# Feed-forward products that stream their columns from last to first

## The chip, the core and the metric

The kernel runs on one core of a Trainium2 chip. Its time is the device time of one execution in microseconds (us). Beside the times there is a profile of one execution: every instruction of the engines TensorE (PE for its products, PEld for the loads of their stationary operand), VectorE (DVE), ScalarE (ACT), GpSimd (POOL) and the queue of SyncE (SP), with its start and its duration, and the DMA transfers.

## The reference

Two steps follow each other. The first is attention over short windows: sequences of 768 positions are cut into chunks of 32, and each chunk attends to 8 memory keys, 16 positions to its left, itself and 8 positions to its right. The second is a feed-forward layer over 3072 tokens with 512 features and 2048 hidden units, in float32:

```python
for c in range(nc):                       # chunks of 32 positions
    k_full = np.concatenate([mem_k, k_ctx], axis=2)
    scores = scale * np.matmul(q_c, k_full.transpose(0, 1, 3, 2))
    ...                                   # softmax: a
    out[:, :, c_start:c_end] = np.matmul(a, v_full)

def _moe_ref(x, w_in, w_out):             # x: 3072 x 512
    h = x @ w_in                          # 3072 x 2048
    g = np.where(h >= 1, h, np.where(h <= -1, 0.0, (h + 1) ** 2 / 4))
    return g @ w_out                      # 3072 x 512
```

## The kernel before

The 3072 tokens are cut into six blocks of 512 (`TB`). The 2048 hidden units are cut into 16 groups of 128, so there are 96 steps, one for each block and group. A step has two sets of products on TensorE:

- the **hidden products** (`pe_hidden`, and the same lines in `early_step`): 128 hidden units of 512 tokens are summed in one PSUM tile `ps_h`. The stationary operand is a 128x128 piece of the weights `wr`, the moving operand is x transposed: 128 features by 512 tokens.
- the **output products** (`pe_products`): the stationary operand is 128x128 of the gated hidden units, `gh` or `gl`, the moving operand 512 columns of `wr`; four tiles `ps_o`, one for each 128 tokens of the block, gather the sum over the 16 groups.

Float32 accuracy comes from splitting each operand in a high part and a remainder (`xth` and `xtl`, `gh` and `gl`, and two halves of `wr`), so that each product is done three times: high by high, high by remainder, remainder by high. A hidden step has 3 x 4 products (4 pieces of 128 features), an output step 3 x 4 (4 tiles of tokens). In the first two blocks some steps are done on half a block: their hidden products have 256 moving columns, and their output steps 6 products.

Between the two sets, ScalarE and VectorE work on one tile of 128x512: two `Relu` and a `Square` on ScalarE, a min-and-add on VectorE, a cast to `gh` on ScalarE and a subtraction to `gl` on VectorE. The output products of a step are issued two steps later (`LAG`). The attention of later blocks (`ps_s` scores, `ps_x` values) is put between the steps, and so is, in the first blocks, the decoding of the packed weights.

All engines run their instructions in the order in which the code issues them (`InOrder`); for the first two blocks this order is the written list `FIRST`, afterwards the loop over steps. All engine calls pass through line 63, so in the profile every instruction has that line, and the groups are told apart by their tiles. In the rows, `ps_h<-xth,wr` and `ps_h<-xtl,wr` are hidden products, `ps_o<-wr,gh` and `ps_o<-wr,gl` output products. Of the kernel's products, `ps_s`, `ps_x`, the transposes `ps_h<-ident,pr` and eight products on zeros at the start (`ps_h<-warm`) are issued by other lines.

Of the kernel before, what the change touches and what calls it, by code (L numbers as in the profile page):

```python
# [16 lines left out]
P = 128  # L17
# [32 lines left out]
"""  # L50

LAST = 2


class InOrder:
# [13 lines left out]
def attn_ffn_kernel(ctx: ExitStack, tc: tile.TileContext, first_qk, first_v, qk, vw, w, out):  # L69
    nc = tc.nc  # L70
    engines = (nc.tensor, nc.scalar, nc.vector, nc.gpsimd, nc.sync)
    pe, act, dve, pool, sp = (InOrder(tc, e) for e in engines)
# [6 lines left out]
    NFC = NPW  # L79
# [14 lines left out]
    def two_banks(tag, name):  # L94
        return ps_2.tile([P, 2, 512], F32, name=name, tag=tag)
# [43 lines left out]
    def weights(which, fc, part):  # L139
        i, j = place[which, fc]  # L140
        c0 = part * n2 + j * DM
        return ws[i][:, c0 : c0 + DM]
# [250 lines left out]
    def hidden_terms(wh, wl, xh, xl):  # L393
        return [(m, x, cc) for m, x in ((wh, xh), (wl, xh), (wh, xl)) for cc in range(NP)]

    def pe_products(outs, gh, gl, wh, wl, fc):

        kinds = list(enumerate(((gh, wh), (gh, wl), (gl, wh))))
        todo = [(t, kind) for kind in kinds for t in range(len(outs))]
        if fc == NFC - 1:  # L400
            todo.sort(key=lambda x: x[0])
        for t, (i, (g, m)) in todo:
            ts = slice(t * P, (t + 1) * P)
            pe.matmul(outs[t], g[:, ts], m, start=fc == 0 and i == 0, stop=fc == NFC - 1 and i == 2)

    def pe_hidden(s):
        blk, fc = divmod(s, NFC)
        xh, xl = xts[blk]
        hp = hidden[s] = ps_h.tile([P, 512], F32, name="ps_h")
        wh, wl = weights(0, fc, 0), weights(0, fc, 1)  # L410
        terms = hidden_terms(wh, wl, xh, xl)
        for n, (m, x, cc) in enumerate(terms):
            pe.matmul(hp, m[:, cc * P : (cc + 1) * P], x[:, cc], start=n == 0, stop=n == len(terms) - 1)

    def gating(s):

# [24 lines left out]
    def pe_out(s):  # L441
        blk, fc = divmod(s, NFC)
        gh, gl = gs.pop(s)
        if fc == 0:
            pairs = [two_banks(f"a{i}", "ps_o") for i in range(NT // 2)]
            acc[blk] = [pairs[t // 2][:, t % 2] for t in range(NT)]
        wh, wl = weights(1, fc, 0), weights(1, fc, 1)
        pe_products(acc[blk], gh, gl, wh, wl, fc)
# [3 lines left out]
    def early_step(name, blk, tokens, fc):  # L452

        items.append(name)
        size = len(tokens) * P
        xh, xl = (x[:, :, tokens[0] * P : tokens[0] * P + size] for x in xts[blk])
        n = 0
        if size < TB:
            n = len(halves) % 2
            halves.append(name)  # L460
        hp = ps_h.tile([P, 512], F32, name="ps_h")[:, 0:size]
        wh, wl = weights(0, fc, 0), weights(0, fc, 1)
        terms = hidden_terms(wh, wl, xh, xl)
        for i, (m, x, cc) in enumerate(terms):
            pe.matmul(hp, m[:, cc * P : (cc + 1) * P], x[:, cc], start=i == 0, stop=i == len(terms) - 1)
        yield
        if n == 0:
            tiles = (
                gpool.tile([P, TB], F32, name="gw", tag="gw"),
                gpool.tile([P, TB], F32, name="gt"),  # L470
                gpool.tile([P, TB], F32R, name="gh", bufs=3),
                gpool.tile([P, TB], F32R, name="gl", bufs=3),
            )
            if size < TB:
                both["g"] = tiles
        else:
            tiles = both["g"]
        g, t, gh, gl = (x[:, n * HT : n * HT + size] for x in tiles)
        act.activation(g, hp, AF.Relu, bias=0.5, scale=0.5)
        act.activation(t, hp, AF.Relu, bias=-1.0)  # L480
        act.activation(g, g, AF.Square)
        yield
        dve.scalar_tensor_tensor(g, g, 1.0, t, op0=ALU.min, op1=ALU.add)
        yield
        act.copy(gh, g)
        yield
        dve.tensor_tensor(gl, g, gh.bitcast(F32), op=ALU.subtract)
        yield
        if fc == 0:
            acc.setdefault(blk, [None] * NT)  # L490
            pair = two_banks(f"a{tokens[0] // 2}", "ps_o")
            for t in tokens:
                acc[blk][t] = pair[:, t % 2]
        wh, wl = weights(1, fc, 0), weights(1, fc, 1)
        pe_products([acc[blk][t] for t in tokens], gh, gl, wh, wl, fc)
        yield
        if fc < NFC - 1:
            return
        for t in tokens:
            if t % 2 == 0:  # L500
                ob = apool.tile([P, 2, DM], F32, name="ob", tag="f", bufs=2)
            (act.copy if t % 2 else dve.tensor_copy)(ob[:, t % 2], acc[blk][t])
            r0 = blk * TB + t * P
            sp.dma_start(out[r0 : r0 + P, :], ob[:, t % 2])
            yield
# [45 lines left out]
    for name in FIRST.split():  # L551
        if name == "+":
            load, *which = next(early)
            load(*which)
            continue
        if name not in chains:
            kind, i = name[0], int(name[1:])
            chains[name] = early_step(name, *parts[kind], i) if kind in parts else kinds[kind](i)
        next(chains[name])
# [13 lines left out]
    for s in range(first * NFC, steps):  # L573
# [22 lines left out]
        if k_scores is not None:  # L596
            act.activation(prob[k_scores], prob[k_scores], AF.Exp, scale=SCALE)
        pe_hidden(s)
        gating(s)
        if s - LAG >= first * NFC:  # L600
# [3 lines left out]
        else:  # L604
            n, i = LAST // LAG, s - first * NFC
            for name in items[len(items) - LAST :][i * n : (i + 1) * n]:
                for _ in chains[name]:
# [96 lines left out]
```

## Time and profile before

| what | value |
|---|---|
| three runs | 608.14, 608.02, 608.13 us (median 608.13) |
| span of the profiled execution, first to last instruction | 606.4 us |
| its time outside the span | no row gives it; the median of the runs lies 1.7 us above the span |
| PE, busy | 591.0 us (97% of the span), 5496 products |
| PEld, busy | 483.7 us (80%) |
| DVE, busy | 325.6 us (54%) |
| ACT, busy | 281.2 us (46%) |
| mean granted TensorE clock | 0.986 |

A product's row on PE has its duration from start to modelled end, and the products of a stream overlap: the mean duration is longer than the distance from one start to the next. The pace of a stream is therefore read from the timeline, from the start of one group of products to the start of the next, divided by their number. In a timeline row the first number is the start, the second the length of the merged piece, and the last the number of instructions.

### The profile page before, as it was taken

The numbers are of one execution on the slowest core, as the hardware profiler recorded it, in microseconds if no ns is written. First come the engines' busy times: TensorE is split into PE (matmuls) and PEld (weight loads), VectorE is DVE, ScalarE is ACT, GpSimd is POOL, SyncE is SP. The second block draws the span as 40 slices with busy tenths as digits, with TensorE's granted clock in tenths as the row PEclk, the third lists the DMA queues.
The fourth block names the chain that finished last, engine by engine and source line by source line (L and its number), as shares of the span: only waits on it lengthen the run. The fifth ranks groups of instructions, "written<-read, shape, count | busy, mean of one in ns | idle before, by whom it ended". The sixth has DMA issues, their size and how long they took to land.

```text
span 606.4 us, 12265 instructions
## 1 busy us (share of the span) xinstructions
PE 591.0 (97%) x5496; PEld 483.7 (80%) x5496; DVE 325.6 (54%) x466; ACT 281.2 (46%) x503; POOL 0.7 (0%) x6
## 2 busy tenths in 40 slices
PE   5889999999999999999999999999999999999996
PEld 2888888888888888888888888888888888888885
DVE  5999999987483224736424734623553632322222
ACT  2689764544444434344434434434433343533342
POOL 0000000000000000000000000000000000000000
PEclk8699999999999999999999999999999999999999
DMA  8999200433131004012201213101310000100001
GB/s 353 423 418 420 124 1 1 175 110 137 31 145 70 1 0 175 30 42 105 70 1 73 103 70 106 70 1 54 121 70 2 1 2 0 70 0 1 0 1 69
DMA packets 9845, 55.31 MB, mean 91 GB/s; under 512 B 1089, under 2 KB 1089, under 8 KB 5185
## 3 DMA queue, kind: packets, MB, share of 16 engines
q1 hardware_dynamic: 9792, 54.53, 23.2%
q8 instruction: 43, 0.70, 0.5%
q14 instruction: 10, 0.07, 0.0%
HBM read 48.23 MB, written 6.29 MB: 90 GB/s over the span
## 4 chain that ended last, share of the span: by engine, by line
PE 94%; DVE 3%; ACT 1%; DMA 1%; issue 0%; DVEq 0%; ACTq 0%
PE ps_o L63 44%; PE ps_h L63 44%; PE ps_x L63 3%; PE ps_s L63 3%; DVE f L63 1%; DMA qk<-in_first_qk_dram 1%; DVE pr L63 1%; DVE mx L63 0%; DVE den L63 0%; ACT w L63 0%; ACT gw L63 0%; DVE wr L63 0%; DVE xtl L63 0%; ACT pr L63 0%; ACT wr L63 0%
## 5 line engine op out<-in xcount | busy, mean ns | idle before, releaser
L63 PE MATMUL ps_o<-wr,gh 128*128 128x512 f32 x768 | 199.5, 396 | 0.0
L63 PE MATMUL ps_h<-xth,wr 128*128 128x512 f32 (+1 forms) x832 | 197.3, 379 | 0.0
L63 PEld LDWEIGHTS ps_h<-xth,wr 128*128 128x128 f32 x832 | 148.7, 189 | 31.9 <-DVE wr L63 0.5
L63 PEld LDWEIGHTS ps_o<-wr,gh 128*128 128x128 f32 x768 | 143.7, 188 | 32.5
L63 DVE SCALAR_TENSOR_TENSOR gw<-gw,gt 128x512 f32<-128x512 f32 (+1 forms) x104 | 67.2, 648 | 170.0 <-ACT gw L63 169.5
L63 ACT ACTIVATE gw<-ps_h 128x512 f32<-128x512 f32 (+1 forms) x104 | 58.7, 564 | 167.8 <-PE ps_h L63 167.7
L63 PE MATMUL ps_o<-wr,gl 128*128 128x512 f32 x384 | 109.0, 394 | 0.0
L63 PE MATMUL ps_h<-xtl,wr 128*128 128x512 f32 (+1 forms) x416 | 105.2, 375 | 0.0
L63 DVE TENSOR_TENSOR gl<-gw,gh 128x512 fp32r<-128x512 f32 (+1 forms) x104 | 67.4, 649 | 67.4 <-ACT gh L63 67.3
L63 ACT CAST gh<-gw 128x512 fp32r<-128x512 f32 (+1 forms) x104 | 61.1, 590 | 68.7 <-DVE gw L63 68.7
L63 PEld LDWEIGHTS ps_h<-xtl,wr 128*128 128x128 f32 x416 | 75.3, 190 | 14.1
L63 PEld LDWEIGHTS ps_o<-wr,gl 128*128 128x128 f32 x384 | 72.5, 189 | 17.2
L63 ACT ACTIVATE gw<-gw 128x512 f32<-128x512 f32 (+1 forms) x104 | 62.5, 601 | 0.0
L63 ACT ACTIVATE gt<-ps_h 128x512 f32<-128x512 f32 (+1 forms) x104 | 58.2, 559 | 0.0
L63 DVE STREAM_TRANSPOSE pt<-pr 32x512 f32<-32x512 f32 (+1 forms) x60 | 41.2, 698 | 1.3
L63 DVE SCALAR_TENSOR_TENSOR f<-w,f 128x1024 uint32<-128x1024 uint32 x32 | 38.9, 1220 | 0.4
L63 PEld LDWEIGHTS ps_x<-pt,v 64*64 64x64 f32 x1536 | 25.2, 142 | 5.5 <-issue 3.5
L63 ACT ACTIVATE pr<-pr 128x1024 f32<-128x1024 f32 (+1 forms) x14 | 13.1, 937 | 35.5 <-DVE pr L63 35.4
L63 PE MATMUL ps_x<-pt,v 64*64 64x32 f32 x1536 | 26.7, 226 | 1.6 <-ACT pt L63 1.6
L63 ACT CAST xth<-ps_x 128x512 fp32r<-128x512 f32 x24 | 13.1, 590 | 21.6 <-PE ps_x L63 21.5
L63 PEld LDWEIGHTS ps_s<-qk 64*32 64x32 f32 x1536 | 16.7, 110 | 6.4 <-issue 3.2
L63 ACT CAST wr<-f 128x1024 fp32r<-128x1024 f32 x16 | 16.8, 1050 | 9.3 <-DVE f L63 9.3
(27 smaller groups left out, 182.1 us busy)
## 6 DMA issues: line engine op xcount, KB each, us to landing
w<-in_w_dram SPq DMA_DIRECT2D x16, 1024.0 KB, 19.8
qk<-in_qk_dram SPq DMA_DIRECT2D x10, 1536.0 KB, 6.7
v<-in_vw_dram SPq DMA_DIRECT2D x10, 1024.0 KB, 5.1
out_dram<-ob SPq DMA_DIRECT2D x24, 256.0 KB, 2.0
qk<-in_first_qk_dram SPq DMA_DIRECT2D x4, 768.0 KB, 8.8
v<-in_first_v_dram SPq DMA_DIRECT2D x4, 512.0 KB, 12.8
```

Of the source, the lines that this page charges most:

```text
L63: return self.tc.keep_in_program_order(getattr(self.engine, name)(*args, **kwargs))
```

## The change

A helper `products` issues a product with the columns of the moving operand in descending order, and with the columns of the PSUM output in the same descending order. Column c of the output is still the product with column c of the moving operand. The hidden products (both places) and the output products go through it; the stationary operand is read as before. The instructions of every engine, their order and their waits are the same in both kernels; the two access patterns of each of these products start at the last column and have the step -1 instead of 1. Lines below the helper move down by five, so that line 63 becomes line 68.

```diff
+def products(pe, out, stationary, moving, **flags):
+
+    pe.matmul(out[:, ::-1], stationary, moving[:, ::-1], **flags)
+
+
...
 def pe_products(outs, gh, gl, wh, wl, fc):
...
-            pe.matmul(outs[t], g[:, ts], m, start=fc == 0 and i == 0, stop=fc == NFC - 1 and i == 2)
+            products(pe, outs[t], g[:, ts], m, start=fc == 0 and i == 0, stop=fc == NFC - 1 and i == 2)
...
 def pe_hidden(s):
...
-            pe.matmul(hp, m[:, cc * P : (cc + 1) * P], x[:, cc], start=n == 0, stop=n == len(terms) - 1)
+            products(pe, hp, m[:, cc * P : (cc + 1) * P], x[:, cc], start=n == 0, stop=n == len(terms) - 1)
...
 def early_step(name, blk, tokens, fc):
...
-            pe.matmul(hp, m[:, cc * P : (cc + 1) * P], x[:, cc], start=i == 0, stop=i == len(terms) - 1)
+            products(pe, hp, m[:, cc * P : (cc + 1) * P], x[:, cc], start=i == 0, stop=i == len(terms) - 1)
```

## The prediction, as written before the result

> **What bounds the kernel now.** I read the page's first part, then the chain of work that ended last, then what PE waits for. Rows of the page:
>
> ```profile
> span 606.4 us, 12265 instructions
> PE 591.0 (97%) x5496; PEld 483.7 (80%) x5496; DVE 325.6 (54%) x466; ACT 281.2 (46%) x503; POOL 0.7 (0%) x6
> PE 94%; DVE 3%; ACT 1%; DMA 1%; issue 0%; DVEq 0%; ACTq 0%
> PE ps_o L63 44%; PE ps_h L63 44%; PE ps_x L63 3%; PE ps_s L63 3%; DVE f L63 1%; DMA qk<-in_first_qk_dram 1%; DVE pr L63 1%; DVE mx L63 0%; DVE den L63 0%; ACT w L63 0%; ACT gw L63 0%; DVE wr L63 0%; DVE xtl L63 0%; ACT pr L63 0%; ACT wr L63 0%
> ```
>
> The chain is PE for 94% of the span, and the two tiles that the change touches, `ps_o` and `ps_h`, hold 88% of it. PE's waits, as the view of waits lists them in full:
>
> ```profile
> PE ps_h L63 <- DVE pr L63: 6.6, 3, 4.1
> PE ps_x L63 <- ACT pt L63: 1.6, 1, 1.6
> PE ps_s L63 <- DMA qk<-in_first_qk_dram: 1.4, 3, 0.8
> PE ps_h L63 <- DVE warm L63: 1.2, 1, 1.2
> ```
>
> Together they are 10.8 us, and none of them is in front of a feed-forward product: `ps_h <- DVE pr` is the transposes of attention, which also land in `ps_h`. So whatever a feed-forward product gains or loses in pace goes into the time in full. The windows of 100 us show the same from the other side:
>
> ```profile
> core 0: us, PE busy (x) PEld busy (x) DVE busy (x) ACT busy (x) POOL busy (x), PEclk, DMA share, GB/s
> 200.00:300.00 100.00, 100.00 (x913) 81.36 (x912) 45.82 (x65) 41.37 (x74) 0.00 (x0) 1.00 0.18 64
> 400.00:500.00 100.00, 100.00 (x913) 81.33 (x913) 45.41 (x65) 41.41 (x75) 0.00 (x0) 1.00 0.11 38
> ```
>
> PE is never idle there, at the full granted clock (1.00), while DVE and ACT are busy less than half of the time and DMA less than a fifth. The other engines could follow products that were 2% faster, and they are covered by products that are slower.
>
> **The pace of a product** is the quantity that the change can move. One late step in the timeline of PE, and one early stretch with the attention out of the way:
>
> ```profile
> 490.50 2.01 PE L63 MATMUL ps_h<-xth,wr 128*128 128x512 f32 x8
> 492.35 1.08 PE L63 MATMUL ps_h<-xtl,wr 128*128 128x512 f32 x4
> 493.26 2.03 PE L63 MATMUL ps_o<-wr,gh 128*128 128x512 f32 x8
> 495.13 1.09 PE L63 MATMUL ps_o<-wr,gl 128*128 128x512 f32 x4
> 496.06 0.40 PE L63 MATMUL ps_h<-xth,wr 128*128 128x512 f32 x1
> ```
>
> ```profile
> 45.50 1.11 PE L63 MATMUL ps_h<-xth,wr 128*128 128x256 f32 x8
> 46.45 0.64 PE L63 MATMUL ps_h<-xtl,wr 128*128 128x256 f32 x4
> 46.93 0.39 PE L63 MATMUL ps_o<-wr,gh 128*128 128x512 f32 x1
> ...
> 51.10 1.98 PE L63 MATMUL ps_h<-xth,wr 128*128 128x512 f32 x8
> 52.92 1.08 PE L63 MATMUL ps_h<-xtl,wr 128*128 128x512 f32 x4
> 53.83 1.10 PE L63 MATMUL ps_o<-wr,gh 128*128 128x512 f32 x4
> ```
>
> From start to start: 12 late hidden products take 493.26 - 490.50 = 2.76 us, 230.0 ns each; 12 late output products 496.06 - 493.26 = 2.80 us, 233.3 ns each. The 12 hidden products from 51.10 take 2.73 us, 227.5 ns each, the fastest stretch of this shape that I found. Twelve products of 256 columns take 46.93 - 45.50 = 1.43 us, 119.2 ns each. Between 256 and 512 columns lie 227.5 - 119.2 = 108.3 ns, so a column costs 108.3 / 256 = 0.423 ns, and what doesn't grow with the columns is 227.5 - 512 x 0.423 = 10.9 ns. A product is thus 95% stream of columns. The counts come from the groups by shape, the loads of the stationary operand beside them:
>
> ```profile
> L63 PE MATMUL ps_o<-wr,gh 128*128 128x512 f32 x768 | 199.5, 396 | 0.0
> L63 PE MATMUL ps_h<-xth,wr 128*128 128x512 f32 x704 | 178.3, 395 | 0.0
> L63 PE MATMUL ps_o<-wr,gl 128*128 128x512 f32 x384 | 109.0, 394 | 0.0
> L63 PE MATMUL ps_h<-xtl,wr 128*128 128x512 f32 x352 | 94.7, 391 | 0.0
> L63 PE MATMUL ps_h<-xth,wr 128*128 128x256 f32 x128 | 19.1, 294 | 0.0
> L63 PE MATMUL ps_h<-xtl,wr 128*128 128x256 f32 x64 | 10.5, 288 | 0.0
> L63 PEld LDWEIGHTS ps_h<-xth,wr 128*128 128x128 f32 x832 | 148.7, 189 | 31.9 <-DVE wr L63 0.5 <-issue 0.2
> L63 PEld LDWEIGHTS ps_o<-wr,gh 128*128 128x128 f32 x768 | 143.7, 188 | 32.5
> ```
>
> That is 1152 output products, 1056 hidden products of 512 columns and 192 of 256. By the late paces they take 1152 x 233.3 = 268.8 us, 1056 x 230.0 = 242.9 us and 192 x 119.2 = 22.9 us, together 534.6 us: 88% of the span, as the chain has it. So the paces describe the whole run. The load of 188 or 189 ns does not set them: the 256-column products follow each other every 119.2 ns with loads of the same kind, so a load's duration overlaps its neighbours.
>
> **The change part by part.** It adds no instruction, removes none, moves none, and moves no wait: the order on each engine is the same row for row. The stationary operand is loaded as before (no cost). What differs in 2400 products is the direction in which columns are read from SBUF and written to PSUM. Three things can have a price.
>
> First, *the boundary between two products*. Today a hidden product's four pieces of x lie behind one another, so the next product begins where the last one ended, except at every fourth. The output products jump back: four of them in a row read the same 512 columns of `wr`. This is the nearest the trace comes to a price of where a stream begins: 233.3 against 230.0 and 227.5 ns. With the change, all hidden products jump too (from the first column of a piece to the last column of the next). From below the price is a gain of 233.3 - 227.5 = 5.8 ns on output products and 2.5 ns on hidden ones, if the jump in the new direction is free and the small irregularity of the pace goes with it: 1152 x 5.8 + 1056 x 2.5 = 6.7 + 2.6 = 9.3 us. From above I take the fixed part of a product paid once more: 2400 x 10.9 ns = 26.2 us. The value that I take is 0. The output tiles' jump goes along with a change of the PSUM tile at every product, so the difference of 3.3 ns need not be the jump's; and in the 12 products from 51.10 the eight of `xth` take 1.82 us and the four of `xtl` 0.91 us, 227.5 ns each, although the stream jumps back after every fourth.
>
> Second, *the stream itself*. From below, 0 per column: the four products that share a moving operand, operands in 16 weight tiles and x tiles of alternating blocks all stream within 3% of each other, so what counts is how many columns there are. From above: the columns come one by one where now two come in the same time. The nearest row with such a pace is that of the first products of all, bf16 ones on zeros:
>
> ```profile
> 1.19 3.59 PE L63 MATMUL ps_h<-warm 128*128 128x512 bf16 x8 [1.19 <-DVE warm L63]
> L63 PE MATMUL ps_h<-warm 128*128 128x512 bf16 x8 | 3.6, 630 | 1.2 <-DVE warm L63 1.2
> ```
>
> The last of the eight starts 3.59 - 0.63 = 2.96 us after the first, 423 ns apiece or 0.826 ns a column, nearly twice 0.423. At 2208 x 512 + 192 x 256 = 1,179,648 columns, a further 0.826 - 0.423 = 0.403 ns is 475 us, and a further 0.423 ns is 499 us. I take 0: nothing in the rows makes a stream depend on its place, and a step of -1 touches the same words as a step of 1, each once, neighbours after neighbours. But every product in this trace runs upward, so no row measures it, and both ends stay for the chances.
>
> [...]
>
> Third, *who waits for the end*. Nobody reads part of a product's output: ScalarE's first `Relu` follows the last of 12 hidden products, the stores the last output product. The order inside changes nothing for them. Cost 0.
>
> The sum is 0 + 0 + 0 against the profiled span of 606.4 us, which lies 1.7 us under the median of the runs; I carry that distance over. Forecast: 608.1 us.
>
> **The rivals.**
>
> *Descending streams run at half the rate* (the far side: slower). Place: every feed-forward product, on reading x and `wr` or on writing `ps_h` and `ps_o`. Price: 499 us by doubling the column, 475 us by the warm-up row, so 1083 to 1107 us. It decides from the first hidden product near 24 us on, since PE has no idle time in which to hide it. For it: the ascending stream takes 0.423 ns a column, half of the 0.826 ns that TensorE also shows, so two columns are handled in the time of one, and pairing may be built for rising addresses alone. Against: only that pairing by place would work both ways. [...]
>
> *A small cost at each product* (slower). The hidden products lose their run-on from piece to piece and take the output products' pace: 1056 x 3.3 ns = 3.5 us, 611.6 us; with a whole fixed part more for each product, 26.2 us, 634.3 us. For it: output products, which jump at every boundary, are the slower kind. Against: the early jumps at every fourth hidden product, which cost nothing visible.
>
> *A small gain.* The 3.3 to 5.8 ns by which late products lie above 227.5 come from how a stream meets its surroundings and go away in the other direction: up to 9.3 us, 598.8 us. For it: the same hidden products take 227.5 ns at 51 us and 230.0 ns at 490 us, so these nanoseconds aren't part of the product. Against: nothing says that direction is what they depend on.
>
> *The change does nothing*: both patterns reversed describe the same set of pairs of columns, and if the instruction were normalised, the chip would see the old one. Time 608.1 us; it falls together with the forecast.
>
> **How the numbers follow.** A difference of 0.2%, 1.2 us, is about the least that a measurement of this kernel tells from no change. No measurable difference (with the rival of a change that does nothing): 0.50. Small gain: 0.15. Small cost: 0.15. Half rate: 0.20. Faster is thus 0.15, the same 0.50, slower 0.15 + 0.20 = 0.35. The range from 598 to 634 us holds the first three, 0.80, with the bounds of 598.8 and 634.3; what it leaves out is the half rate. The forecast's own range is 606.9 to 609.3 us.
>
> **What would show it.** If the forecast holds: late steps with 2.76 us for hidden and 2.80 us for output products, mean durations of 391 to 396 ns in the groups, and PE's waits as above. A small cost or gain: the distance of starts in these same late steps, and only there; 256-column products shifted by the same nanoseconds as those of 512 columns if it lies at the boundary, by half as much if it lies in the columns. Half rate: starts some 440 ns apart, loads with gaps of more than 200 ns between them, DVE and ACT near a quarter. The forecast is wrong if the span moves by more than 1.2 us; its reason is wrong if the paces move and cancel.

## The result, and the profile after

The changed kernel takes 612.3 us (612.31 and 612.35, a third run 614.03) where the kernel before takes 608.1. The ratio over all three is 1.0078, with an interval of 1.0064 to 1.0092. Measured again beside the experiments it was 612.35 against 608.15 us, 1.0069 (1.0054 to 1.0084). The change costs 4 us, 0.7%. One run each of this kernel and of the experiments `d2_pad_down` and `b1_read` took 832.33, 832.82 and 652.92 us at granted clocks of 0.65 to 0.84 and is left out of all numbers; the rows below are of a second profile of the changed kernel, `a1_both`.

The page of the changed kernel, span, engines and chain:

```profile
span 610.5 us, 12349 instructions
PE 595.2 (97%) x5496; PEld 483.2 (79%) x5496; DVE 325.8 (53%) x466; ACT 281.4 (46%) x503; POOL 0.7 (0%) x6
PE 94%; DMA 4%; ACT 1%; SPq 0%; issue 0%; DVE 0%; DVEq 0%; ACTq 0%
```

The page counts 84 instructions more than that of the kernel before (12349 against 12265). In the trace they are semaphore instructions of some 51 ns in TensorE's queue, one more in nearly every hidden step. So the instructions of the two kernels are not quite the same, against what the section on the change says. The experiments show that they cost nothing: `b2_write`, `b3_halves` and `b4_fours` have the same 12349 and take the time of the kernel before, while `b1_read` with 12265 and `a3_output` with 12264 have the whole loss.

The span grows by 4.1 us and PE's busy time by 4.2 us. PE's waits are as they were:

```profile
PE ps_h L68 <- DVE pr L68: 6.7, 3, 4.1
PE ps_x L68 <- ACT pt L68: 1.6, 1, 1.6
PE ps_h L68 <- DVE warm L68: 1.2, 1, 1.2
PE ps_s L68 <- DMA qk<-in_first_qk_dram: 1.0, 2, 0.8
```

They sum to 10.5 us against 10.8. So no wait appeared; the products themselves are slower. PE's timeline shows where, in a late step of the changed kernel and 16 steps on:

```profile
504.92 2.03 PE L68 MATMUL ps_h<-xth,wr 128*128 128x512 f32 x8
506.78 1.10 PE L68 MATMUL ps_h<-xtl,wr 128*128 128x512 f32 x4
507.72 2.03 PE L68 MATMUL ps_o<-wr,gh 128*128 128x512 f32 x8
509.58 1.10 PE L68 MATMUL ps_o<-wr,gl 128*128 128x512 f32 x4
510.52 1.80 PE L68 MATMUL ps_h<-xth,wr 128*128 128x512 f32 x7
...
594.52 2.03 PE L68 MATMUL ps_h<-xth,wr 128*128 128x512 f32 x8
```

Hidden and output products both take 2.80 us for twelve: 233.3 ns each. Sixteen steps take 594.52 - 504.92 = 89.60 us, 5.600 us a step. The kernel before, over the same 16 steps:

```profile
501.61 2.01 PE L63 MATMUL ps_h<-xth,wr 128*128 128x512 f32 x8
...
590.46 2.01 PE L63 MATMUL ps_h<-xth,wr 128*128 128x512 f32 x8
```

88.85 us, 5.553 us a step. The 2208 products of 512 columns are worth 2208 / 24 = 92 such steps: 92 x 0.047 = 4.3 us. The products of 256 columns went the other way, a little. Early, in the changed kernel:

```profile
45.42 1.11 PE L68 MATMUL ps_h<-xth,wr 128*128 128x256 f32 x8
46.37 0.64 PE L68 MATMUL ps_h<-xtl,wr 128*128 128x256 f32 x4
46.84 0.63 PE L68 MATMUL ps_o<-wr,gh 128*128 128x512 f32 x2
```

That is 1.42 us for twelve, 118.3 ns each, against 119.2 ns (1.43 us) before: over 192 products 0.2 us less. By these samples 4.3 - 0.2 = 4.1 us, the growth of the span. Summed over all starts in the records, the distances behind hidden products of 512 columns grew by 3.7 us and those behind output products by 0.7 us; those behind products of 256 columns fell by 0.1 us and those behind all others by 0.2 us.

The starts of the single products say more than their mean. The distances from one start to the next in a step of each kernel, the ones from 501.61 and from 504.92 us, in ns, from the records (12 hidden products, then 12 output products):

```
before, hidden   236 224 231 236 228 232 231 227 227 226 227 232
before, output   241 233 231 231 229 230 232 241 232 231 232 233
after,  hidden   234 233 233 234 233 233 234 233 233 234 233 233
after,  output   234 233 233 234 233 233 234 233 233 234 233 233
```

Before, the pace is uneven in the same way in nearly every step; the hidden products settle at 226.7 ns after some seven products, the output products never settle and repeat a pattern of seven with a mean of 232.4. After, every product takes 233.3. The change replaced a mixture with a mean of 231.4 by a constant that is a little worse.

### The profile page after: what moved, and what is told of

Its sections match the earlier page's. It is cut to its first block, busy times and chain, and to the rows that moved or that the text cites. A ratio compares the mean times of both kernels' runs of the same rounds, so it can differ in the third digit from the quotient of the medians.

```text
span 830.5 us, 12349 instructions
## 1 busy us (share of the span) xinstructions
PE 816.0 (98%) x5496; PEld 541.4 (65%) x5496; DVE 327.9 (39%) x466; ACT 281.9 (34%) x503; POOL 0.7 (0%) x6
## 4 chain that ended last, share of the span: by engine, by line
PE 97%; DVE 2%; DMA 1%; ACT 0%; issue 0%; DVEq 0%; ACTq 0%
PE ps_h L68 46%; PE ps_o L68 45%; PE ps_x L68 4%; PE ps_s L68 2%; DMA qk<-in_first_qk_dram 1%; DVE f L68 0%; DVE pr L68 0%; DVE den L68 0%; DVE mx L68 0%; DVE wr L68 0%; DVE ob L68 0%; ACT gw L68 0%; DVE rin L68 0%; ACT pr L68 0%; ACT pt L68 0%
## 5 line engine op out<-in xcount | busy, mean ns | idle before, releaser
L68 PE MATMUL ps_o<-wr,gh 128*128 128x512 f32 x768 | 272.5, 511 | 0.0
L68 PE MATMUL ps_h<-xth,wr 128*128 128x512 f32 (+1 forms) x832 | 269.5, 486 | 0.0
L68 PEld LDWEIGHTS ps_h<-xth,wr 128*128 128x128 f32 x832 | 168.5, 214 | 81.8 <-issue 24.6
L68 PEld LDWEIGHTS ps_o<-wr,gh 128*128 128x128 f32 x768 | 159.7, 209 | 87.8 <-issue 28.0
L68 PE MATMUL ps_o<-wr,gl 128*128 128x512 f32 x384 | 148.3, 503 | 0.0
L68 PE MATMUL ps_h<-xtl,wr 128*128 128x512 f32 (+1 forms) x416 | 143.6, 475 | 0.0
L68 PEld LDWEIGHTS ps_h<-xtl,wr 128*128 128x128 f32 x416 | 83.6, 211 | 42.4 <-issue 14.7
L68 PEld LDWEIGHTS ps_o<-wr,gl 128*128 128x128 f32 x384 | 78.1, 203 | 46.6 <-issue 16.7
L68 PEld LDWEIGHTS ps_x<-pt,v 64*64 64x64 f32 x1536 | 32.5, 176 | 7.0 <-issue 5.1
L68 PE MATMUL ps_x<-pt,v 64*64 64x32 f32 x1536 | 34.0, 245 | 0.9 <-ACT pt L68 0.9
L68 DVE COPY ob<-ps_o 128x512 f32<-128x512 f32 (+1 forms) x16 | 9.6, 622 | 37.9 <-PE ps_o L68 37.9
```

What stands on the lines that cost most here:

```text
L68: return self.tc.keep_in_program_order(getattr(self.engine, name)(*args, **kwargs))
```

## The experiments

### Which products, and where they begin

The first four runs separate the two theories that the prediction left: a price at the boundary between products, or one in the stream. Each kernel is the changed one with one edit. `a1_both` is the changed kernel itself.

> The changed kernel itself, for a profile at the clock of the kernel before. The boundary theory (each hidden product loses the run-on from one piece of x to the next): +3 to +5 us, the distance of starts in late hidden products up from 230.0 to about 233 to 234 ns, late output products unchanged at 233.3 ns, the attention's products unchanged. The stream theory (each column read or written downward costs a little more): about 1.8 ns more on every 512-column product, 231.8 ns hidden and 235.1 ns output, and 0.9 ns more on those of 256 columns.

Measured: 612.35 us, the rows above. Hidden products at 233.3 ns fit the boundary theory, and so do output products, whose mean is unchanged; but the 256-column products became faster, which fits neither.

`a2_hidden`:

```diff
 def pe_products(outs, gh, gl, wh, wl, fc):
-            products(pe, outs[t], g[:, ts], m, ...)
+            pe.matmul(outs[t], g[:, ts], m, ...)
```

> Only the hidden products run downward; output products upward as before. Boundary theory: the whole loss, +3 to +5 us. Stream theory: the share of the hidden products' columns, 590,000 of 1,180,000, so half the loss, about +2.1 us.

Measured: 612.2 us (one of four runs 613.66), ratio 1.0072 (1.0057 to 1.0087). The hidden products alone bring the whole loss.

`a3_output`: `products` in `pe_products` only, `pe.matmul` in both hidden places.

> Only the output products run downward. Boundary theory: no loss, within 0.5 us of the kernel before, because their stream already jumps at each boundary. Stream theory: half the loss, about +2.1 us.

Measured: 613.0 us, ratio 1.0079 (1.0062 to 1.0096). The output products alone bring the whole loss too. Both theories miss: one wanted 0, the other 2.1 us. The step of this run on PE:

```profile
505.45 2.01 PE L68 MATMUL ps_h<-xth,wr 128*128 128x512 f32 x8
507.30 1.08 PE L68 MATMUL ps_h<-xtl,wr 128*128 128x512 f32 x4
508.22 2.06 PE L68 MATMUL ps_o<-wr,gh 128*128 128x512 f32 x8
510.11 1.11 PE L68 MATMUL ps_o<-wr,gl 128*128 128x512 f32 x4
511.06 0.39 PE L68 MATMUL ps_h<-xth,wr 128*128 128x512 f32 x1
```

Here the downward output products take 2.84 us for twelve, 236.7 ns, where the same products take 233.3 when the hidden ones run downward too. The losses do not add up: 4.1 and 4.9 us apart, 4.2 together.

`a4_pieces`, the changed kernel with:

```diff
-    ... for cc in range(NP)]
+    ... for cc in reversed(range(NP))]
```

> All products run downward as in the changed kernel, and the four pieces of x are taken from the last to the first, so that a downward hidden product ends where the next one begins, as the upward ones do in the kernel before. The sums are the same with another order of terms. Boundary theory: the loss is gone, within 0.5 us of the kernel before. Stream theory: the same loss as the changed kernel, +4 to +5 us.

Measured: 612.36 us, 1.0069 (1.0054 to 1.0084), the same loss, although each downward hidden product but every fourth now ends where the next one begins. The boundary theory falls.

### Reading or writing, and what "downward" means

`b1_read` and `b2_write` turn only one side of each product:

```diff
-    pe.matmul(out[:, ::-1], stationary, moving[:, ::-1], **flags)
+    pe.matmul(out, stationary, moving[:, ::-1], **flags)      # b1_read
+    pe.matmul(out[:, ::-1], stationary, moving, **flags)      # b2_write
```

> The moving operands are read downward, the outputs written upward. The columns of each product therefore land mirrored (tokens within a block, features in the output), with the same number of products and words; that part of the result is another one. Read theory (the price lies in reading SBUF downward, together with the load of the next stationary operand from the same memory): the whole loss, +4 us, 233.3 ns in late hidden and output products, evenly. Write theory (the price lies in writing PSUM downward): the time of the kernel before, with its uneven paces (226 to 241 ns).

> The moving operands are read upward as in the kernel before, the outputs written downward, so that columns land mirrored as well. Read theory: the time of the kernel before and its uneven paces. Write theory: +4 us with 233.3 ns evenly. If each gives half of it, neither holds.

Measured: reading downward 612.43 us, 1.0071 (1.0054 to 1.0088); writing downward 608.07 us, 1.0000 (0.9990 to 1.0009). The price lies in reading alone. In the run that writes downward, a step has the distances of the kernel before within 1 ns (the one from 501.55 us begins 236 224 231 236 228 233 230 227). So writing the output with a step of -1 cost nothing here.

`b3_halves` takes the second half of the columns first, each half upward; `b4_fours` turns the columns inside each group of four (16 bytes), the groups upward:

```diff
+    a, b = (x.rearrange("p (h c) -> p h c", c=n)[:, ::-1] for x in (out, moving))     # b3_halves, n = half
+    a, b = (x.rearrange("p (h c) -> p h c", c=4)[:, :, ::-1] for x in (out, moving))  # b4_fours
+    pe.matmul(a, stationary, b, **flags)
```

> Read and written upward, but the second half of the columns ahead of the first, by one instruction with two runs of columns. If the direction decides (step -1 from column to column), this keeps the time and the pace of the kernel before, but for a jump in the middle. If the place decides at which a stream is while the next stationary operand is loaded, the pace changes as much as in the changed kernel, by 3 ns or more a product.

> Groups of four columns (16 bytes) go upward, and inside each group the columns go downward, in reading and in writing. If the step from word to word decides, the loss of the changed kernel stays, +4 us, or more. If only the large order decides (which part of the operand is read when), the kernel takes the time of the kernel before. If a turn inside a group costs time, which neither kernel has, the stream slows by tens of ns a product and the time by 50 us or more.

Measured: 608.11 us, 1.0000 (0.9991 to 1.0010), and 608.14 us, 0.9999 (0.9990 to 1.0009). In `b4_fours` every single step from word to word inside a group is -1, and it costs nothing. So it isn't the step of words inside 16 bytes that has a price: with the groups of 16 bytes in downward order as well the kernel takes 612.35 us.

### The pace of single kinds of products

To ask many such questions at once, `c1_probe` is the kernel before with 26 stretches of 36 products each behind its end (819.4 us in all), `c2_probe` the same in the opposite order (820.9 us). The core of a stretch, shortened; `offset` counts columns of 4 bytes:

```python
for i in range(36):
    a = i % 3
    s = wh[:, a * 128 : a * 128 + cols]                  # or wh[:, ::4]
    m = xh[:, a * 512 + offset : a * 512 + offset + n]
    pe.matmul(hp[0:cols, 0:n], s, order(m), start=True, stop=True)
```

> The kernel before, and behind its last product 26 stretches of 36 products each, whose results nobody reads; only their pace is asked, from start to start, and the whole time is longer by them. Each stretch changes one thing: the direction of the moving operand, the number of columns of the stationary operand (128, 64, 32), the number of moving columns (512, 256), the address of the moving operand (later by 16, 64 or 256 bytes), a stationary operand taken from every fourth word, groups of columns turned round (inside groups of 16, 64 and 256, or groups of 4, 16 and 64 in downward order), bf16 operands. Collision theory (a downward stream meets the load of the next stationary operand in SBUF more often): 226.7 ns up and 233.3 ns down at 128 stationary columns, the difference below 2 ns at 32 columns, whose load is a quarter; other paces with the strided load, and with at least one of the shifted addresses. Own-price theory (a downward product pays some 6.7 ns by itself, whatever is loaded beside it): the same difference of 6 to 7 ns at 128, 64 and 32 columns, in bf16 too, and no effect of the stride and the addresses.

> The same 26 stretches in the opposite order. If the pace of a stretch belongs to the stretch, each has the pace that it had in the other order within 1 ns. If it depends on what went before, as the output products' pace seems to (233.3 ns where the hidden products run downward too, 236.7 ns where they run upward), some of them change by 3 ns or more.

Measured, mean of the last 24 distances of starts of each stretch in ns, from the records of both runs; the two runs agree within 0.1 ns (where the trace lacks a record, as it does in one bf16 stretch of each run, the other run's number stands), so a stretch's pace is its own and not its predecessor's:

| stretch (512 columns, 128 stationary columns where not said) | up | down |
|---|---|---|
| plain | 226.7 | 233.3 |
| the same operands every time | 226.7 | 233.3 |
| 64 stationary columns | 230.0 | 233.3 |
| 32 stationary columns | 231.7 | 233.3 |
| stationary operand from every fourth word | 235.0 | 233.3 |
| moving operand 16 bytes later | 231.7 | 233.3 |
| moving operand 64 bytes later | 228.9 | 233.3 |
| moving operand 256 bytes later | 226.7 | 233.3 |
| 256 moving columns | 120.0 | 118.3 |
| bf16 | 215.8 | 215.8 |

| order of the columns | |
|---|---|
| inside groups of 4 downward (from `b4_fours`) | as up |
| inside groups of 16 downward, groups upward | 266.7 |
| inside groups of 64 or 256 downward, groups upward | 233.3 |
| groups of 4 or of 16 in downward order, upward inside | 233.3 |
| groups of 64 in downward order, upward inside | 226.7 |

Rows of PE's timeline in `c1_probe`, upward: part of the plain stretch, then of the one whose stationary operand is every fourth word:

```profile
602.27 6.97 PE L63 MATMUL ps_h<-xth,wr 128*128 128x512 f32 x30
...
732.80 5.57 PE L63 MATMUL ps_h<-xth,wr 128*128 128x512 f32 x23
```

Less 0.39 and 0.40 us for the last product's own duration, 29 distances of the first row take 6.58 us, 226.9 ns each (its first ones are not settled), and 22 of the second 5.17 us, 235.0 ns.

Three things follow. First, the upward pace is not a property of the product alone: it goes from 226.7 to 235.0 ns when only the stationary operand changes (every fourth word; with 64 or 32 columns, 230.0 and 231.7 ns, the output has fewer rows as well) and to 231.7 or 228.9 ns when only the moving operand's address does (16 or 64 bytes later). The difference of 6.7 ns falls to 1.7 at 32 columns, as the collision theory said, yet not in the way that it said: up becomes slower, down stays. So it is no simple count of meetings with a shorter load, and the load of a quarter of the columns was not a quarter as long: 109 ns against 188. Nor is it the length of the load alone: every fourth word takes 309 ns to load beside upward products and 312 ns beside downward ones, whose pace stays at 233.3 ns. Second, in these stretches the downward pace of 512 columns is 233.3 ns with every stationary operand and address that was tried; in the kernel of `a3_output` it was 236.7. Third, with groups in downward order but upward inside, groups of 4 and 16 columns have the downward pace, 233.3 ns, and groups of 64 (256 bytes) the upward one, 226.7 ns. Groups of 32 columns were not tried, and groups of 16 turned inside, at 266.7 ns, have neither pace.

bf16 products show no difference, in the one place that was tried: 215.8 ns in either direction. In float32 a change of the stationary operand alone moved the upward pace from 226.7 to 235.0 ns; what the product loses there, no run shows.

### The shift that beats both kernels

The stretches suggest a reason for the output products' uneven 232.4 ns in the kernel before. In the built programs' addresses, x and the weights begin at 1664 modulo 2048, so that a hidden product's two operands lie whole multiples of 512 bytes apart, the distance of the plain stretch. The tiles of `gh` and `gl` begin at 0 modulo 2048, 128 bytes off. `d1_pad_up` puts 128 unused bytes ahead of their pool; `d2_pad_down` does the same in the changed kernel:

```diff
+    gpool.tile([P, 32], F32, name="pad", bufs=1)
     warm = gpool.tile([P, DM], BF16, name="warm", tag="gw")
```

> The kernel before, products upward, with 128 unused bytes ahead of the pool that holds gh and gl. In the kernel before, those tiles begin 128 bytes off a multiple of 512 from the weights, while x and the weights lie whole multiples of 512 bytes apart. Collision theory (the upward pace hangs on where the moving operand and the next stationary operand lie to one another): the output products settle at 226.7 ns instead of their uneven 232.4, and the hidden products behind them have no slow start; 1152 x 5.7 = 6.6 us and up to 1056 x 3 = 3.2 us less, 598 to 602 us. Own-price theory, and any theory in which the output products are slower because they change the PSUM tile: no change, 608.1 us.

> The changed kernel, products downward, with the same 128 bytes. Collision theory as the stretches bear it out (every downward stretch settled at 233.3 ns, whatever its addresses): 612.3 us, no change against the changed kernel. If the downward pace hangs on the addresses as well, it moves by 3 us or more.

Measured: upward with the shift 600.09 us, ratio 0.9871 (0.9856 to 0.9886), faster than both kernels; downward with the shift 612.37 us, 1.0069 (1.0055 to 1.0083), nothing gained. The step of `d1_pad_up`:

```profile
501.08 1.98 PE L63 MATMUL ps_h<-xth,wr 128*128 128x512 f32 x8
502.90 1.07 PE L63 MATMUL ps_h<-xtl,wr 128*128 128x512 f32 x4
503.80 1.98 PE L63 MATMUL ps_o<-wr,gh 128*128 128x512 f32 x8
505.62 1.07 PE L63 MATMUL ps_o<-wr,gl 128*128 128x512 f32 x4
506.52 0.39 PE L63 MATMUL ps_h<-xth,wr 128*128 128x512 f32 x1
```

A step takes 5.44 us: both kinds of products run at 226.7 ns from the first to the last, the slow start of the hidden ones is gone with the output products' uneven pace, and the change of the PSUM tile at every output product costs nothing.

The 128 bytes also say which place matters. In the stretches only the moving operand was shifted; here the output products' moving operand `wr` lies where it lay, and only their stationary operand moved (with `gw` and `gt`, which no product reads). Both shifts change the pace (226.7 to 231.7 ns by 16 bytes there, 232.4 to 226.7 ns here), so it does not hang on the place of one of them alone; that where the two lie to one another decides is the reading that fits both.

By the steps the gain would be 92 x (5.553 - 5.44) = 10.4 us; the span fell by 8.0. Not every step of the kernel before was as slow as the late ones: the twelve hidden products from 51.10 us took 227.5 ns each. Summed over the records, the distances behind output products fell by 6.7 us, behind hidden products by 1.8 us, and behind all others they grew by 0.5 us. The page of `d1_pad_up`:

```profile
span 598.4 us, 12265 instructions
PE 581.7 (97%) x5496; PEld 482.7 (81%) x5496; DVE 325.6 (54%) x466; ACT 280.5 (47%) x503; POOL 0.7 (0%) x6
PE 87%; DVE 6%; DMA 4%; issue 1%; ACT 1%; SPq 0%; DVEq 0%; ACTq 0%
```

Its waits have one row in front of feed-forward products, which the kernel before did not have:

```profile
PE ps_h L63 <- DVE wr L63: 1.0, 1, 1.0
```

PE's busy time fell by 9.3 us, and its idle time grew from 606.4 - 591.0 = 15.4 to 16.7 us: in the first blocks PE now waits once for VectorE's decoding (`wr`). VectorE's 6% of the chain, 3% before, says nothing more: in `b4_fours`, which takes the time of the kernel before, it is 14%.

### How far apart

Left open was whether downward has a good distance that the four tried had missed.

> The kernel before, and behind its last product 22 stretches of 36 products of 512 columns, up and down in turn, whose results nobody reads. The moving operand begins 0, 32, 64, 96, 128, 160, 192, 224, 256, 384 and 512 bytes behind a multiple of 512 bytes from the stationary one. Collision theory: upward 226.7 ns at 0, 256 and 512 bytes, more at the distances between (the kernel before has 128 bytes in its output products, 232.4 ns); if downward collides at a constant rate, 233.3 ns at every distance. If downward has a good distance of its own, one of these eleven shows less than 230 ns, and the changed kernel could be brought below the kernel before by a shift.

Measured (793.5 us in all), mean of the last 24 distances in ns, from the records; "bytes" is how far the moving operand lies from a multiple of 512 bytes from the stationary one:

| bytes | 0 | 32 | 64 | 96 | 128 | 160 | 192 | 224 | 256 | 384 | 512 |
|---|---|---|---|---|---|---|---|---|---|---|---|
| up | 226.7 | 233.3 | 228.9 | 233.3 | 233.3 | 234.2 | 233.3 | 233.3 | 226.7 | 233.3 | 226.7 |
| down | 233.3 | 233.3 | 233.3 | 233.3 | 233.3 | 233.3 | 233.3 | 233.3 | 233.3 | 233.3 | 233.3 |

The first two stretches and the one at 96 bytes upward, in PE's timeline (each row begins with the first start in the window; it holds 31 or 29 products of one stretch):

```profile
602.66 7.19 PE L63 MATMUL ps_h<-xth,wr 128*128 128x512 f32 x31
...
611.30 6.93 PE L63 MATMUL ps_h<-xth,wr 128*128 128x512 f32 x29
...
671.29 6.92 PE L63 MATMUL ps_h<-xth,wr 128*128 128x512 f32 x29
```

Less the last product's own duration, 0.39 us upward and 0.40 us downward, 30 distances of the first row take 6.80 us, 226.7 ns each; 28 of the second and of the third take 6.53 us, 233.2 ns each. None of the eleven distances is good for downward, 233.3 ns at each; for upward 0, 256 and 512 bytes are, at 226.7 ns, and 64 is in between at 228.9. At 128 bytes, the distance of the output products in the kernel before, the stretch has 233.3 ns and the kernel 232.4: near, but not the same.

The mean granted clock of this run is 1.000. That of `c1_probe` is 1.00 throughout its stretches, which show the same 226.7 and 233.3 ns:

```profile
core 0: us, PE busy (x) PEld busy (x) DVE busy (x) ACT busy (x) POOL busy (x), PEclk, DMA share, GB/s
600.00:700.00 100.00, 100.00 (x484) 74.16 (x483) 2.20 (x4) 0.96 (x2) 0.00 (x0) 1.00 0.03 11
700.00:815.00 115.00, 114.88 (x506) 91.03 (x507) 0.00 (x0) 0.00 (x0) 0.00 (x0) 1.00 0.00 1
```

So 233.3 ns is a pace at a granted clock of 1.00. The rows of `a1_both` have the same pace at a mean granted clock of 0.936 (0.95 from 400 to 500 us), and further runs of that kernel took 612.31 and 612.38 us at 0.985 where its own took 612.29. The loss is none of the clock's.

## Why the prediction was wrong

- **What bounds the kernel** held for the loss. PE is 94% of the chain, nothing covers a product, and the change of the distances gave the 4.1 us of the span. For a gain it holds less: in `d1_pad_up` a wait of 1.0 us for decoding appeared ahead of hidden products.
- **No instruction added** was false, by 84 semaphore instructions in TensorE's queue, and cost nothing (`b2_write` has them, at 608.07 us).
- **The distances** held as numbers and were read too coarsely. I took 227.5, 230.0 and 233.3 ns as one pace with a small irregularity that might or might not have a cause. The single starts, which the records had, show a settled pace of 226.7 ns and a pattern that repeats every seven products. A pace that varies in so regular a way has a cause, and the direction was one thing that it could hang on.
- **The boundary**, taken at 0: 0 is right (`a4_pieces`, 612.36 us), and the bound of a fixed part paid again was never reached.
- **The stream**, taken at 0: this is the step that failed. "Nothing in the rows makes a stream depend on its place" passed over rows that I had: hidden and output products differ in the place of their operands, and their paces differed by 3 to 6 ns. I put that down to the PSUM tile or to nothing; in `d1_pad_up`, where only the place was changed, both run at 226.7 ns. By the distances of a step shown above the term measured (233.3 - 229.8) x 1056 = 3.7 us on hidden products, 229.8 being the mean of the twelve before, and (233.3 - 233.0) x 1152 = 0.3 us on output products (0.7 us over the whole run). What costs it is reading the moving operand downward (`b1_read`, 612.43 us), not writing the output (`b2_write`, 608.07 us). Nor is it a price per column, as I had bounded the term: the products of 256 columns did not lose half as much but became faster (118.3 against 119.2 ns).
- **A step of -1 touches the same words**, neighbours after neighbours: inside 16 bytes it cost nothing (`b4_fours`, 608.14 us), over the whole operand 4 us (`a1_both`, 612.35 us).
- **Half rate** did not come: the widest difference by direction is 6.7 ns on 226.7, 3%, not 100%. The row that priced it, 423 ns for a bf16 product at the start of the kernel, is no pace of that shape either: in the probe such products took 215.8 ns in both directions, near the 226.7 of float32, so it does not show that two float32 columns are handled in the time of one.
- **A small cost at each product** came nearest, 611.6 us for 612.3, and half of its test held: the late steps' starts moved, but not only there, since twelve hidden products at 51 us went from 2.73 to 2.80 us. Its mechanism fell, so that the near number is luck. The hidden products did take the output products' pace of 233.3 ns, but with the run-on restored they kept it (`a4_pieces`), and turning the output products alone cost as much (`a3_output`). Its other test failed too: the 256-column products became faster by about 1 ns, where a price at the boundary or in the columns would have made them slower.
- **A small gain**, 598.8 us if all products ran at 227.5 ns: the reasoning was right that those nanoseconds are no part of the product, and wrong on what takes them away. That is not the direction but a shift of 128 bytes, with 600.1 us.
- **Who waits for the end**: nobody, as said; no wait of another kind appeared in the changed kernel.

What stays open: *why* the distance matters. That the load and the reading of the moving operand disturb one another was my theory; it fits that changing the stationary operand alone moves the upward pace from 226.7 to 235.0 ns, but no run shows it. Why upward is slower with a shorter load (231.7 ns beside loads of 109 ns, 226.7 beside 188), why groups of 16 turned inside cost 266.7 ns, and why the downward output products took 236.7 ns in `a3_output` and 233.3 in the changed kernel, was not settled; the stretches show no such memory of what went before, but their output stays in one PSUM tile.

## What to carry to other kernels

Where float32 products follow one another without a gap, look at the distances of single starts, not only at the pace of groups: a pattern that repeats from step to step is a reason to try a shift of the operands' places. Let the moving operand be read upward, and try it at a distance of 0, 256 or 512 bytes from the stationary operand that is loaded beside it, counted from a multiple of 512 (226.7 ns here, against 228.9 to 234.2 at the other eight distances); 128 unused bytes took 1.3% off this kernel. Writing the PSUM columns downward (608.07 us) and turning the words inside 16 bytes (608.14 us) were free, against 608.15 us.

## What the runs showed of the hardware that I had not expected

- In the stretches a float32 product of 512 columns takes 226.7 to 235.0 ns from start to start, depending on direction, address and the load beside it, where bf16 takes 215.8 in either direction.
- In the stretches downward reading of the moving operand gives 233.3 ns at every one of eleven distances and with loads of 128, 64 and 32 columns; upward reading gives 226.7 only at three of the eleven, 0, 256 and 512 bytes.
- With a stationary operand of 32 columns the upward products were slower than with 128 (231.7 against 226.7 ns).
- Columns turned inside groups of 16 (64 bytes) cost 40 ns a product, 266.7 against 226.7, while groups of 64 or 256 turned inside cost 6.7, and groups of 4 nothing (608.14 us in `b4_fours`).
- Products of 256 columns were faster downward: 118.3 against 120.0 ns in the stretches.
